# Attention and sticky-expert kernel: gate loads behind batch 0's keys, a sparse read of batch 0's keys and values at the start, batch 2's keys behind its phi

## The chip, the core and the metric

One core of one Trainium2 chip runs the kernel. The time is the device time of one execution in microseconds; of several executions the median is given. A profiled execution has a span (first to last instruction) and a time of its own that also holds what lies around the span.

## What is computed

Eight batches, eight heads, 576 tokens, head width 64, 32 memory slots; eight experts with a hidden width of 1024.

```python
a = softmax(phi, over the 576 tokens)               # [b, h, s, 32]
k_m = einsum('bhsm,bhsd->bhmd', a, k)               # 32 keys and 32 values for each head
v_m = einsum('bhsm,bhsd->bhmd', a, v)
attn = softmax(q @ k_m.T / 8)                       # [b, h, s, 32]
x = (attn @ v_m)                                    # heads side by side: [b, s, 512]
# sticky experts: token 0 takes argmax(x @ w_gate); a later token takes a fresh argmax
# where sigmoid(x @ w_local) < 0.5, else the expert of the token before
out[b, s] = p[e] * (relu(x[b, s] @ w1[e]) @ w2[e])
```

## The kernel before

The work goes batch by batch. For one batch there is an attention part (softmax of `phi`, the products with keys and values, the scores of the queries) and an expert part: the logits of the batch's first token choose one expert (`c_pl`, `c_choice`, L860 to L881), the index goes to the queue that issues transfers (`expert`, L1342), its `w1` and `w2` are loaded, `w_pg` (L1065) multiplies the batch's 32 values with `w1`, `hidden` (L1094) and `second`, `second_turned` (L1129, L1187) do the two large products. Tokens with another expert are done at the end, if there are any.

The order on every engine is written by hand. `SCHEDULE` (L41) is a list of steps, "batch name"; its first line (L42) is everything before batch 0's large products, and each later line is run at one `yield` of `moe`, so after a group of large matmuls of the batch that is then in its expert part. A step appends its instructions to the engines' queues, and each engine works in that order. In the expert part of one batch the attention part of the next is interleaved.

All transfers are issued by SyncE (SP in the profile) in the order of the steps; a transfer that has to wait for its buffer holds up what is behind it in that queue. The buffers that matter: `kv_t` (keys and values of a batch, one buffer), `q_t` (one), `phi_t` (one, and batch 1's in another place), `raw` (halves of `w1` and `w2`, three).

Steps that the change and the prediction name, with their lines:

- `phi`: 576 KB (L468); for batch 0 in two pairs of heads, `phi 0` and `phi 1`, of 288 KB (L1463). `colmax` (L561, work in L559) takes the maximum over tokens, `pm`, `mc`, `pm2`, `cx` (L593 to L618) spread it, `sub` and `exp` (L620, L625) give the weights.
- `k 0`, `v 0`, `v 1`, `k 1`: batch 0's keys and values in pieces of six and three of nine token groups (L476, `PIECES` in L450, issued by L466). `kv tile` allocates the buffer, `kv` allocates it and loads keys and values, `k` and `v` load one of them.
- `pkv a`, `pkv b` (batch 0) and `pkv 0`, `pkv 1` (L646): the products of weights with keys and values. They read keys and values together, six and three token groups in batch 0.
- `gate loads` (L413): `w_local` as 4 rows of 512 bytes into `wl`, and `w_gate` into `wg`, in pieces of 32 bytes. `gate turn` (L417): one small transpose of `wl` on TensorE and one copy into `wg` on ScalarE. `wg` is first read by `pgg` (L714).
- `fill N`, `warm`: matmuls on zeros whose result nobody reads (L535, L550).
- `q 0`, `q 1`: half the heads of a batch's queries, eight transfers of 72 KB in rows of 128 bytes (L483). `q0 b`, `q0 c`: batch 0's queries (L525).
- `w1 0`, `w1 1`, `w2 0`, `w2 1`: halves of the expert's matrices (L1031, L1043). `pg 0` needs `w1 0` and `pg 1` needs `w1 1`; `G 0`, `G 1` (L1084) split the products in two parts of lower precision on ScalarE and VectorE for `hidden`.

Of the kernel before, what the change touches and what calls it, by code (L numbers as in the profile page):

```python
# [8 lines left out]
F32 = mybir.dt.float32  # L9
# [29 lines left out]
}  # L39

SCHEDULE = """  # L41
1 warm s, 0 gate constants, 0 kv tile, 0 q0 tile, 1 warm s, 1 warm t, 0 fill 0, 0 warm f, 0 q0 a, 1 warm s, 0 phi 0, 0 phi 1, 0 colmax 0, 0 gate loads, 0 warm f, 0 k 0, 0 colmax 1, 0 pm, 0 mc, 0 warm b, 0 pm2, 0 cx, 0 dsub 0, 0 dsub 1, 0 v 0, 0 v 1, 0 exp 0, 0 exp 1, 0 warm f, 0 k 1, 0 asum 0, 0 warm f, 0 o q, 1 phi, 0 fill 7, 0 pkv a, 0 gate turn, 0 asum 1, 0 fill 1, 0 sums, 0 fill 2, 0 pkv b, 0 rinv, 0 q0 b, 0 kvn, 0 fill 3, 0 pT, 0 kvT, 0 fill 4, 0 o psc, 1 kv tile, 1 cm 0, 0 pgg, 0 o turn, 0 o mx, 0 o sub, 0 warm b, 0 o exp, 0 p q 0, 0 o sum, 0 at, 0 o inv, 0 o mul, 1 cm 1, 0 o at, 0 ggt, 0 p q 1 0, 0 p q 1 1, 0 q0 c, 0 pl0, 1 k, 1 cm 2, 0 choice, 0 fill 5, 0 p psc, 0 p turn, 0 p mx, 0 p sub 0, 0 z q 0, 0 fill 6, 0 p sub 1, 0 q0 d, 0 expert, 0 p exp 0, 0 p sum 0, 1 pm, 0 p exp 1, 0 p sum 1, 0 p inv, 0 z q 1, 0 z q 2, 0 w1 0 a, 1 mc, 0 p mul 1, 0 p at 1, 0 pg lo, 1 pm2, 0 p mul 0, 0 p ah 1, 0 Gh lo 0, 0 z psc, 0 p at 0, 0 p ah 0, 0 Gh lo 1, 0 w1 1, 1 cx, 0 Gl lo, 0 p al 1, 1 v, 0 z turn, 0 p al 0, 0 fill 9, 1 sub 1, 1 sub 0, 0 z mx  # L42
0 pg hi, 0 pg 1, 0 G hi, 0 z sub, 0 G 1, 1 exp 0, 0 z exp, 1 exp 1, 1 asum, 0 w2 0, 0 z sum, 1 q 0, 0 warm b
0 w2 1, 0 z inv, 0 z mul, 0 z at

# [8 lines left out]


0 split 5, 0 split 6, 1 z qT 1, 0 at store
2 phi, 0 g exp, 1 kvT, 1 a psc, 0 split 7, 1 pgg
1 a turn
0 g prob
1 a mx, 0 g cols, 1 a sub, 2 colmax  # L60
# [1 line left out]
2 pm, 2 mc  # L62
1 ggt, 0 evict 1
1 z psc, 1 a at, 1 z turn, 1 pl0, 1 a ah
1 choice, 1 a al, 2 kv, 2 pm2, 1 z mx, 1 z sub, 1 expert
2 z qT 0, 2 cx, 1 z exp
1 z sum
1 w1 0, 1 z inv
# [59 lines left out]
4 kv, 3 z sub, 3 expert, 3 w1 0, 4 asum, 3 z exp, 3 z sum  # L128
2 g cols, 3 z inv
3 z mul  # L130
3 z at, 2 g present, 4 a qT 0, 1 kv store, 4 q 1, 4 pkv 0, 3 w1 1, 4 pkv 1, 5 phi, 3 w2 0, 3 pg 0, 5 q 0, 4 sums, 3 g pl, 3 z ah
3 g lt, 2 evict 0, 4 rinv, 4 z qT 0, 3 g L

3 G 0, 4 kvn, 4 z qT 1, 3 z al, 4 a qT 1, 4 pT
4 kvT, 4 a psc, 2 evict 1, 3 g fresh, 4 a turn, 4 a mx, 3 pg 1, 4 pgg, 5 colmax, 4 a sub, 4 ggt, 3 g kept
# [197 lines left out]
def tile_memattn_stickymoe(  # L333
# [12 lines left out]
    nc = tc.nc  # L346
# [13 lines left out]
    const = ctx.enter_context(tc.tile_pool(name="const", bufs=1))  # L360
# [40 lines left out]
    def gate_constants():  # L401
        for e in range(E):
            nc.gpsimd.memset(code[:, e : e + 1], float(E - e))
        for i in range(2):
            nc.gpsimd.memset(ggts[i], 0.0)
            nc.gpsimd.memset(ams[i], 0.0)
            nc.gpsimd.memset(ends[i], 0.0)
            nc.gpsimd.memset(crs[i], 0.0)
            nc.gpsimd.memset(c0s[i], 0.0)
# [51 lines left out]
    def load_tokens(dst, src, heads, piece=slice(0, TN)):  # L461

        m = src.shape[2]
        ns = slice(m * piece.start, m * piece.stop)
        sv = src.rearrange("(h g) (p n) m -> (g p) h (n m)", g=NG, n=TN)
        nc.sync.dma_start(out=dst[:, heads].rearrange("p h n m -> p h (n m)")[:, :, ns], in_=sv[:, heads, ns])  # L466

    def fetch_phi(st, by_pairs=False, pool=pin, tag="phi"):  # L468
        st.pt = pool.tile([P, HG, TN, M], F32, tag=tag, name="phi_t", bufs=1)
        for hs in pairs if by_pairs else (slice(0, HG),):  # L470
            load_tokens(st.pt, phi[st.b], hs)

    def kv_tile(st):
        st.kv = pin.tile([P, 2, HG, TN, D], F32, tag="kv", name="kv_t", bufs=1)
# [864 lines left out]
    h, w = pairs  # L1339
    a, z = PARTS  # L1340
# [21 lines left out]
    def al(st, p):  # L1362
# [4 lines left out]
    STEPS = {  # L1367

        "phi": lambda st: fetch_phi(st) if st.b > 1 else fetch_phi(st, False, pf, "oT"),
        "kv": fetch_kv,  # L1370
        "kv tile": kv_tile,
# [89 lines left out]
    lo, hi = slice(0, 256), slice(256, 512)  # L1461

    def phi_pair(st, hs):  # L1463
# [4 lines left out]
    STEPS.update({  # L1468

        "gate loads": gate_loads,  # L1470
        "gate turn": gate_turn,
        "gate constants": lambda st: gate_constants(),
        "warm f": lambda st: warm(1, 1024),
# [110 lines left out]
```

## Time and profile before

| | us |
|---|---|
| median of 3 runs | 395.77 (393.54 to 396.47) |
| the profiled execution's own time | 396.51 |
| its span | 394.9 |
| TensorE matmuls busy | 385.2 |
| VectorE busy | 280.7 |
| ScalarE busy | 177.1 |
| GpSimd busy | 152.6 |

The granted TensorE clock is at full speed in the whole span. The profiled execution is 0.74 us above the median of the runs, and 1.6 us of its time lie around the span. In the rows below, PE is a matmul, PEld the load of its weights (which overlaps matmuls), DVE VectorE, ACT ScalarE, POOL GpSimd, SPq the queue that issues transfers. "Landing" counts from the start of the issue. An engine's idle time stands in brackets before the thing that ended it.

### The profile page before, as it was taken

The numbers are of one execution on the slowest core, as the hardware profiler recorded it, in microseconds if no ns is written. First come the engines' busy times: TensorE is split into PE (matmuls) and PEld (weight loads), VectorE is DVE, ScalarE is ACT, GpSimd is POOL, SyncE is SP. The second block draws the span as 40 slices with busy tenths as digits, with TensorE's granted clock in tenths as the row PEclk, the third lists the DMA queues.
The fourth block names the chain that finished last, engine by engine and source line by source line (L and its number), as shares of the span: only waits on it lengthen the run. The fifth ranks groups of instructions, "written<-read, shape, count | busy, mean of one in ns | idle before, by whom it ended". The sixth has DMA issues, their size and how long they took to land.

```text
span 394.9 us, 10791 instructions
## 1 busy us (share of the span) xinstructions
PE 385.2 (98%) x4326; PEld 333.7 (84%) x4326; DVE 280.7 (71%) x701; ACT 177.1 (45%) x437; POOL 152.6 (39%) x164
## 2 busy tenths in 40 slices
PE   8999999899999999999999999999999999999996
PEld 5667979699898976899879988799888998799886
DVE  3588798888986797875887689747745677356330
ACT  1257742437435565216461752525533653435311
POOL 1025733428125672047513931328513651057000
PEclk9999999999999999999999999999999999999999
DMA  7989979899969887999578847998580039702111
GB/s 216 341 266 272 204 161 361 235 270 224 237 227 288 212 293 184 288 340 230 192 250 230 274 140 246 352 275 216 168 297 4 2 81 325 270 0 66 29 42 57
DMA packets 115950, 82.59 MB, mean 209 GB/s; under 512 B 70132, under 2 KB 89592, under 8 KB 115896
## 3 DMA queue, kind: packets, MB, share of 16 engines
q1 hardware_dynamic: 115896, 81.86, 70.3%
q8 instruction: 35, 0.57, 0.6%
q14 instruction: 19, 0.16, 0.1%
HBM read 66.60 MB, written 15.24 MB: 207 GB/s over the span
## 4 chain that ended last, share of the span: by engine, by line
PE 52%; DMA 5%; SPq 4%; DVE 1%; issue 1%; ACT 1%; DVEq 0%
PE ph L1109 15%; PE po L1147 6%; PE po L1148 5%; PE po L1149 5%; PE po L1197 5%; PE po L1198 5%; PE po L1199 5%; DMA att_d<-at 3%; SPq L492 3%; PE pg L1076 2%; PE pkv L654 2%; DMA raw<-in_moe_w_dram 1%; PE po L1171 1%; PE psc L779 1%; PE pl L889 1%
## 5 line engine op out<-in xcount | busy, mean ns | idle before, releaser
L1062 POOL TENSOR_TENSOR w2l<-raw,w2h 128x512 fp32r<-128x512 f32 x64 | 83.2, 1323 | 59.4 <-ACT w2h L1061 40.9
L1109 PE MATMUL ph<-ah,Gh 128*128 128x256 f32 (+1 forms) x256 | 73.4, 301 | 0.6 <-DVE h L1119 0.5
L1109 PE MATMUL ph<-ah,Gl 128*128 128x256 f32 (+1 forms) x256 | 72.3, 296 | 0.2
L1197 PE MATMUL po<-h,w2l 128*128 128x320 f32 x224 | 71.0, 317 | 0.0
L1119 DVE SCALAR_TENSOR_TENSOR h<-ph,h 128x320 fp32r<-128x320 f32 (+2 forms) x104 | 52.4, 517 | 25.3 <-ACT h L1117 24.7
L1199 PE MATMUL po<-h,w2h 128*128 128x320 f32 x224 | 69.2, 309 | 0.0
L1198 PE MATMUL po<-h,w2h 128*128 128x320 f32 x224 | 69.2, 309 | 0.0
L1117 ACT ACTIVATE h<-ph 128x320 fp32r<-128x320 f32 (+1 forms) x96 | 46.7, 492 | 39.1 <-PE ph L1109 38.9
L1147 PE MATMUL po<-w2h,h 128*128 128x512 f32 (+1 forms) x152 | 58.9, 388 | 0.0
L1148 PE MATMUL po<-w2l,h 128*128 128x512 f32 (+1 forms) x152 | 57.6, 379 | 0.0
L1149 PE MATMUL po<-w2h,h 128*128 128x512 f32 (+1 forms) x152 | 57.5, 378 | 0.0
L1109 PE MATMUL ph<-al,Gh 128*128 128x256 f32 (+1 forms) x256 | 54.9, 295 | 0.0
L1109 PEld LDWEIGHTS ph<-ah,Gh 128*128 128x128 f32 x256 | 48.1, 188 | 2.5 <-DVE h L1119 1.0
L1204 POOL TENSOR_TENSOR oT<-oT,gT 128x320 f32<-128x320 f32 x28 | 21.9, 789 | 72.6 <-DVE oT L1203 56.1
L848 POOL TENSOR_TENSOR al<-at,ah 128x576 fp32r<-128x576 f32 (+1 forms) x18 | 23.1, 1291 | 67.4 <-ACT ah L844 67.4
L1109 PEld LDWEIGHTS ph<-ah,Gl 128*128 128x128 f32 x256 | 48.1, 188 | 0.6 <-DVE Gl L1091 0.6
L1061 ACT ACTIVATE w2h<-raw 128x512 fp32r<-128x512 f32 x64 | 38.1, 625 | 22.7 <-PE po L1199 14.9
L1197 PEld LDWEIGHTS po<-h,w2l 128*128 128x128 f32 x224 | 42.2, 188 | 1.8 <-issue 1.1
L1198 PEld LDWEIGHTS po<-h,w2h 128*128 128x128 f32 x224 | 42.1, 188 | 0.1
L1199 PEld LDWEIGHTS po<-h,w2h 128*128 128x128 f32 x224 | 42.1, 188 | 0.0
L1109 PEld LDWEIGHTS ph<-al,Gh 128*128 128x128 f32 x256 | 41.2, 189 | 0.0
L1147 PEld LDWEIGHTS po<-w2h,h 128*128 128x128 f32 x152 | 28.6, 188 | 6.5 <-issue 1.6
(165 smaller groups left out, 588.4 us busy)
## 6 DMA issues: line engine op xcount, KB each, us to landing
raw<-in_moe_w_dram SPq DMA_DIRECT2D x34, 512.0 KB, 6.6
raw<-in_moe_w_dram SPq DMA_DIRECT2D x15, 1024.0 KB, 7.3
kv_t<-in_k_dram SPq DMA_DIRECT2D x7, 1152.0 KB, 7.4
kv_t<-in_v_dram SPq DMA_DIRECT2D x7, 1152.0 KB, 10.7
q_t<-in_q_dram SPq DMA_DIRECT2D x112, 72.0 KB, 3.5
att_d<-at SPq DMA_DIRECT2D x8, 576.0 KB, 4.3
out_dram<-oT SPq DMA_DIRECT2D x28, 160.0 KB, 3.3
phi_t<-in_phi_dram SPq DMA_DIRECT2D x7, 576.0 KB, 6.3
```

Source lines behind the costliest of these rows:

```text
L848: (eng or nc.gpsimd).tensor_tensor(out=st.al[:, gs, ss], in0=st.at[:, gs, ss], in1=st.ah[:, gs, ss], op=ALU.subtract)
L1061: nc.scalar.activation(h, src, AF.Copy)
L1062: nc.gpsimd.tensor_tensor(out=l, in0=src, in1=h, op=ALU.subtract)
L1109: nc.tensor.matmul(pv[:, c - c0], lhsT=lt[:, g, cs], rhs=rt[:, g, s0 : s0 + n], start=(i == 0), stop=(i == 5),)
L1117: nc.scalar.activation(hc[:, :, 0:n], pv, AF.Relu)
L1119: nc.vector.scalar_tensor_tensor(out=hc[:, :, o : o + z - a], in0=pv[:, :, a:z], scalar=0.0, in1=hc[:, :, a:z], op0=ALU.max, op1=ALU.subtract,
L1147: nc.tensor.matmul(po[:, c0:c1], lhsT=h[:, c, th], rhs=hi, start=(c == 0), stop=False)
L1148: nc.tensor.matmul(po[:, c0:c1], lhsT=h[:, c, th], rhs=lo, start=False, stop=False)
L1149: nc.tensor.matmul(po[:, c0:c1], lhsT=h[:, c, tl], rhs=hi, start=False, stop=(c == FC - 1))
L1197: nc.tensor.matmul(po[:, 0:n], lhsT=lo, rhs=h[:, c, 0:n], start=(c == 0), stop=False)
L1198: nc.tensor.matmul(po[:, 0:n], lhsT=hi, rhs=h[:, c, 0:n], start=False, stop=False)
L1199: nc.tensor.matmul(po[:, 0:n], lhsT=hi, rhs=h[:, c, n : 2 * n], start=False, stop=(c == FC - 1))
```

## The change

Four edits:

1. A new step `touch`, first in the schedule. It issues two transfers from ScalarE's queue: of batch 0's keys, and of its values, 16 bytes out of every 32 KB, 36 rows each, into two small tiles that nothing reads.
2. `gate loads` goes from before `k 0` to behind `k 1`, and `gate turn` from between `pkv a` and `asum 1` to behind `kvn`, ahead of `fill 3`.
3. For batch 2, `kv` is split in `kv tile`, `k` and `v`; the buffer and the keys come right behind `2 phi`, ahead of batch 2's first queries (`2 q 0`), the values stay where `kv` was.
4. For batch 3, `pg 0` goes to the next line of the schedule, so behind `4 sums`, `3 g pl` and one more group of large matmuls.

```diff
 SCHEDULE
-1 warm s, 0 gate constants, 0 kv tile, 0 q0 tile,
+0 touch, 1 warm s, 0 gate constants, 0 kv tile, 0 q0 tile,
...
-0 phi 0, 0 phi 1, 0 colmax 0, 0 gate loads, 0 warm f, 0 k 0, 0 colmax 1,
+0 phi 0, 0 phi 1, 0 colmax 0, 0 warm f, 0 k 0, 0 colmax 1,
...
-0 v 0, 0 v 1, 0 exp 0, 0 exp 1, 0 warm f, 0 k 1, 0 asum 0, 0 warm f, 0 o q, 1 phi, 0 fill 7,
+0 v 0, 0 v 1, 0 exp 0, 0 exp 1, 0 warm f, 0 k 1, 0 gate loads, 0 asum 0, 0 warm f, 0 o q, 1 phi, 0 fill 7,
-0 pkv a, 0 gate turn, 0 asum 1, 0 fill 1, 0 sums, 0 fill 2, 0 pkv b, 0 rinv, 0 q0 b, 0 kvn, 0 fill 3,
+0 pkv a, 0 asum 1, 0 fill 1, 0 sums, 0 fill 2, 0 pkv b, 0 rinv, 0 q0 b, 0 kvn, 0 gate turn, 0 fill 3,
...
-2 phi, 0 g exp, 1 kvT, 1 a psc, 0 split 7, 1 pgg
+2 phi, 2 kv tile, 2 k, 0 g exp, 1 kvT, 1 a psc, 0 split 7, 1 pgg
...
-1 choice, 1 a al, 2 kv, 2 pm2, 1 z mx, 1 z sub, 1 expert
+1 choice, 1 a al, 2 v, 2 pm2, 1 z mx, 1 z sub, 1 expert
...
-3 z at, 2 g present, 4 a qT 0, 1 kv store, 4 q 1, 4 pkv 0, 3 w1 1, 4 pkv 1, 5 phi, 3 w2 0, 3 pg 0, 5 q 0, 4 sums, 3 g pl, 3 z ah
-3 g lt, 2 evict 0, 4 rinv, 4 z qT 0, 3 g L
+3 z at, 2 g present, 4 a qT 0, 1 kv store, 4 q 1, 4 pkv 0, 3 w1 1, 4 pkv 1, 5 phi, 3 w2 0, 5 q 0, 4 sums, 3 g pl, 3 z ah
+3 pg 0, 3 g lt, 2 evict 0, 4 rinv, 4 z qT 0, 3 g L
...
+    def touch():
+        for i, x in enumerate((k, v)):
+            t = const.tile([36, 4], F32, name=f"touch{i}")
+            nc.scalar.dma_start(out=t, in_=x[0].rearrange("h s d -> (h s d)").rearrange("(t x) -> t x", t=36)[:, 0:4])
```

## Rows read from the trace of the kernel before

**Rows 1.** The page: busy time of each engine; the chain that ended last.

```profile
PE 385.2 (98%) x4326; PEld 333.7 (84%) x4326; DVE 280.7 (71%) x701; ACT 177.1 (45%) x437; POOL 152.6 (39%) x164
PE 52%; DMA 5%; SPq 4%; DVE 1%; issue 1%; ACT 1%; DVEq 0%
```

**Rows 2.** Waits of TensorE's weight loads: total us, times, longest.

```profile
PEld pg L1076 <- DMA raw<-in_moe_w_dram: 4.1, 4, 1.8
```

**Rows 3.** Timeline of the issuing queue, first 8 us: start, us, engine, line, transfer.

```profile
2.83 0.41 SPq L414 DMA_DIRECT2D wl<-in_moe_w_local_dram  x1
3.71 0.50 SPq L466 DMA_DIRECT2D kv_t<-in_k_dram  x1
```

**Rows 4.** Transfers issued in the first 80 us: count, KB each, us to landing.

```profile
wg<-in_moe_w_gate_dram SPq DMA_DIRECT2D x1, 16.0 KB, 4.4
kv_t<-in_v_dram SPq DMA_DIRECT2D x1, 768.0 KB, 7.6
kv_t<-in_k_dram SPq DMA_DIRECT2D x1, 384.0 KB, 8.8
```

**Rows 5.** Windows of the start: length, busy by engine, clock, DMA share, GB/s.

```profile
2.75:4.75 2.00, 2.00 (x41) 1.48 (x38) 0.00 (x0) 0.00 (x0) 0.03 (x1) 1.00 0.88 261
4.75:6.75 2.00, 2.00 (x23) 1.08 (x22) 1.94 (x2) 0.00 (x0) 0.00 (x0) 1.00 0.91 177
6.75:9.75 3.00, 2.83 (x11) 1.14 (x10) 1.27 (x3) 0.28 (x1) 0.00 (x0) 1.00 1.05 383
```

**Rows 6.** Timeline of the engines, 4 to 14 us.

```profile
4.81 2.17 DVE L559 TENSOR_REDUCE cm<-phi_t 128x64 f32<-128x576 f32 x2 [3.36 <-DMA phi_t<-in_phi_dram]
...
8.69 0.28 ACT L618 ACTIVATE cx<-pm 128x128 f32<-128x128 f32 x1 [6.49 <-PE pm L612]
...
10.85 0.89 PE L555 MATMUL wp<-wz 128*128 128x32 bf16 x21
11.96 1.58 PE L654 MATMUL pkv<-kv_t,phi_t 64*32 64x128 f32 x96 [0.22 <-DMA kv_t<-in_v_dram]
...
13.48 0.13 PEld L420 LDWEIGHTS pwl<-ident,wl 4*128 4x128 f32 x1 [0.20 <-issue]
```

**Rows 7.** Timeline of the issuing queue, 48 to 65 us.

```profile
52.97 4.49 SPq L492 DMA_DIRECT2D q_t<-in_q_dram  x8
57.55 0.44 SPq L466 DMA_DIRECT2D kv_t<-in_k_dram  x1
58.04 0.51 SPq L466 DMA_DIRECT2D kv_t<-in_v_dram  x1
64.02 1.03 SPq L1040 DMA_DIRECT2D raw<-in_moe_w_dram  x2
```

**Rows 8.** Windows around these transfers, columns as in rows 5.

```profile
53.00:54.00 1.00, 1.00 (x6) 0.81 (x5) 0.96 (x4) 0.00 (x0) 0.15 (x1) 1.00 0.09 29
54.00:59.00 5.00, 5.00 (x24) 4.12 (x23) 4.86 (x11) 2.70 (x10) 0.00 (x0) 1.00 0.80 124
```

**Rows 9.** Landing of batch 2's values (issued 58.04) and batch 1's `w1 0` (64.02).

```profile
kv_t<-in_v_dram SPq DMA_DIRECT2D x1, 1152.0 KB, 9.1
raw<-in_moe_w_dram SPq DMA_DIRECT2D x1, 1024.0 KB, 7.3
```

**Rows 10.** Timeline of weight loads and VectorE, 65 to 78 us.

```profile
65.48 0.74 DVE L747 STREAM_TRANSPOSE qT<-q_t 128x576 f32<-128x576 f32 x1
...
71.31 0.18 PEld L1076 LDWEIGHTS pg<-raw,kvT 64*32 64x32 f32 x16 [1.80 <-DMA raw<-in_moe_w_dram]
...
73.12 1.29 DVE L1091 TENSOR_TENSOR Gl<-pg,Gh 128x512 fp32r<-128x512 f32 x2 [1.54 <-ACT Gh L1089]
```

**Rows 11.** Timeline around batch 3's `pg 0` and `pg 1`: weight loads, issuing queue.

```profile
152.71 0.18 PEld L1076 LDWEIGHTS pg<-raw,kvT 64*32 64x32 f32 x16 [1.12 <-DMA raw<-in_moe_w_dram]
...
161.18 0.18 PEld L1076 LDWEIGHTS pg<-raw,kvT 64*32 64x32 f32 x16 [0.69 <-DMA raw<-in_moe_w_dram]
...
155.23 0.40 SPq L1040 DMA_DIRECT2D raw<-in_moe_w_dram  x1
```

More of the change, by code (lines that the diff above doesn't have):

```diff
@@ L41 @@
 SCHEDULE = """
-1 warm s, 0 gate constants, 0 kv tile, 0 q0 tile, 1 warm s, 1 warm t, 0 fill 0, 0 warm f, 0 q0 a, 1 warm s, 0 phi 0, 0 phi 1, 0 colmax 0, 0 gate loads, 0 warm f, 0 k 0, 0 colmax 1, 0 pm, 0 mc, 0 warm b, 0 pm2, 0 cx, 0 dsub 0, 0 dsub 1, 0 v 0, 0 v 1, 0 exp 0, 0 exp 1, 0 warm f, 0 k 1, 0 asum 0, 0 warm f, 0 o q, 1 phi, 0 fill 7, 0 pkv a, 0 gate turn, 0 asum 1, 0 fill 1, 0 sums, 0 fill 2, 0 pkv b, 0 rinv, 0 q0 b, 0 kvn, 0 fill 3, 0 pT, 0 kvT, 0 fill 4, 0 o psc, 1 kv tile, 1 cm 0, 0 pgg, 0 o turn, 0 o mx, 0 o sub, 0 warm b, 0 o exp, 0 p q 0, 0 o sum, 0 at, 0 o inv, 0 o mul, 1 cm 1, 0 o at, 0 ggt, 0 p q 1 0, 0 p q 1 1, 0 q0 c, 0 pl0, 1 k, 1 cm 2, 0 choice, 0 fill 5, 0 p psc, 0 p turn, 0 p mx, 0 p sub 0, 0 z q 0, 0 fill 6, 0 p sub 1, 0 q0 d, 0 expert, 0 p exp 0, 0 p sum 0, 1 pm, 0 p exp 1, 0 p sum 1, 0 p inv, 0 z q 1, 0 z q 2, 0 w1 0 a, 1 mc, 0 p mul 1, 0 p at 1, 0 pg lo, 1 pm2, 0 p mul 0, 0 p ah 1, 0 Gh lo 0, 0 z psc, 0 p at 0, 0 p ah 0, 0 Gh lo 1, 0 w1 1, 1 cx, 0 Gl lo, 0 p al 1, 1 v, 0 z turn, 0 p al 0, 0 fill 9, 1 sub 1, 1 sub 0, 0 z mx
+0 touch, 1 warm s, 0 gate constants, 0 kv tile, 0 q0 tile, 1 warm s, 1 warm t, 0 fill 0, 0 warm f, 0 q0 a, 1 warm s, 0 phi 0, 0 phi 1, 0 colmax 0, 0 warm f, 0 k 0, 0 colmax 1, 0 pm, 0 mc, 0 warm b, 0 pm2, 0 cx, 0 dsub 0, 0 dsub 1, 0 v 0, 0 v 1, 0 exp 0, 0 exp 1, 0 warm f, 0 k 1, 0 gate loads, 0 asum 0, 0 warm f, 0 o q, 1 phi, 0 fill 7, 0 pkv a, 0 asum 1, 0 fill 1, 0 sums, 0 fill 2, 0 pkv b, 0 rinv, 0 q0 b, 0 kvn, 0 gate turn, 0 fill 3, 0 pT, 0 kvT, 0 fill 4, 0 o psc, 1 kv tile, 1 cm 0, 0 pgg, 0 o turn, 0 o mx, 0 o sub, 0 warm b, 0 o exp, 0 p q 0, 0 o sum, 0 at, 0 o inv, 0 o mul, 1 cm 1, 0 o at, 0 ggt, 0 p q 1 0, 0 p q 1 1, 0 q0 c, 0 pl0, 1 k, 1 cm 2, 0 choice, 0 fill 5, 0 p psc, 0 p turn, 0 p mx, 0 p sub 0, 0 z q 0, 0 fill 6, 0 p sub 1, 0 q0 d, 0 expert, 0 p exp 0, 0 p sum 0, 1 pm, 0 p exp 1, 0 p sum 1, 0 p inv, 0 z q 1, 0 z q 2, 0 w1 0 a, 1 mc, 0 p mul 1, 0 p at 1, 0 pg lo, 1 pm2, 0 p mul 0, 0 p ah 1, 0 Gh lo 0, 0 z psc, 0 p at 0, 0 p ah 0, 0 Gh lo 1, 0 w1 1, 1 cx, 0 Gl lo, 0 p al 1, 1 v, 0 z turn, 0 p al 0, 0 fill 9, 1 sub 1, 1 sub 0, 0 z mx
 0 pg hi, 0 pg 1, 0 G hi, 0 z sub, 0 G 1, 1 exp 0, 0 z exp, 1 exp 1, 1 asum, 0 w2 0, 0 z sum, 1 q 0, 0 warm b
@@ L1470, in tile_memattn_stickymoe @@
         "gate loads": gate_loads,
+        "touch": lambda st: touch(),
         "gate turn": gate_turn,
```

## The prediction

> **What bounds the kernel now.** I read the page first. TensorE's matmuls are busy for 98% of the span, and the chain that ended last is TensorE for more than half of its length, with transfers and the issuing queue for 9% [rows 1]. So a gain is only a place where TensorE stands still, or where it does work that nobody needs. The second view is the waits of the weight loads: TensorE's largest wait for another unit is `pg` for its `w1`, 4.1 us in four pieces, the longest 1.80 us [rows 2]. The third is the timeline, at the three places where the diff works: the first 15 us [rows 3 to 6], the time around batch 1's `pg 0` [rows 7 to 10], and batch 3's `pg 0` and `pg 1` [rows 11]. The reader is to see in each which wait ends last, and what stands right behind it.
>
> **Edits 1 and 2, the start.** Batch 0's chain is: phi lands, `colmax` starts at 4.81 as its wait for phi ends, and from there every step waits for the one before until `pkv a`; in between TensorE, between short links of the chain, does a fixed string of fills, whose last ends at 10.85 + 0.89 = 11.74. `pkv a` starts at 11.96, the 0.22 us between put down to the landing of `v 0` [rows 6], which takes 7.6 us [rows 4].
>
> The transfers have a hole. From 4.75 to 6.75 the core moves 177 GB/s, in the 3 us after that 383 [rows 5]. At 383 the same bytes would have taken 2.0 x 177 / 383 = 0.92 us, so 1.08 us are lost, just where the gate's 32-byte pieces and the first reads of `k 0` stand in the queue. Edit 2 takes the two gate transfers from there, and 3.71 - 2.83 = 0.88 us of the queue's time [rows 3]; edit 1 is aimed at the first reads. How the hole divides between them no row tells. I don't need to know: if all of it goes, `v 0` lands about 1.1 us earlier, before 10.9, but the fills end at 11.74. The load can give back 0.22 us and not more, and a fifth of the hole is enough for that.
>
> `gate turn` leaves the place between `pkv a` and `pkv b`. It costs 0.13 us there, with the 0.20 us of issue before it 0.33 at most [rows 6]; I take 0.13, since issue pauses stand before the next instruction too. `pkv b` can use it if `k 1` is there; that has the longest landing of the start, 8.8 us [rows 4], and any part of the hole brings it nearer. At its new place, behind `kvn`, TensorE waits for `kvn` anyway, and `wg` is not read before `pgg`, some 2 us later. The gate transfers now stand behind `k 1` and ahead of batch 1's phi in the queue. `w_gate` took 4.4 us [rows 4]; from an issue 3 to 4 us later than now it lands by 12, or with `k 1` near 14, and `gate turn`, behind `pkv b` and so after 14 us, is read late enough. Nothing else in that queue changes place; batch 1's phi and batch 0's queries are issued at the times of before. Start: 0.22 + 0.13 = 0.35 us.
>
> The two reads are issued from ScalarE, which has nothing to do before 8.69 (6.49 us idle, [rows 6]). The trace has no transfer from ScalarE; the nearest rows are SP's issues of small rows, 0.41 us each [rows 3], so two take 0.8 us, and even at the 4.49 / 8 = 0.56 us of a query transfer [rows 7] they are over long before 8.69. Nothing, then, on that engine. What they do to the transfers beside them is not shown; phi's 576 KB are moving at 261 GB/s from 2.75 to 4.75 [rows 5], and phi is what the chain waits for. The bounds: nothing, if a read costs an engine only its bytes (72 x 16); 1.08 us if the whole lost time of the hole moves ahead of phi; 4.4 us if phi ends as late as a transfer like the gate's, landing behind the two reads. I take nothing, the row nearest in bytes being far from filling the engines, and keep 1.08 and 4.4 for the rivals.
>
> [...]
>
> **Edit 3, batch 2's keys.** Batch 1's `pg 0` stands at 71.31 after 1.80 us of wait for `w1 0` [rows 10]. That transfer was issued at 64.02 and landed 7.3 us later, at 71.3; before it in the queue stand batch 2's values, issued at 58.04, landing at 58.04 + 9.1 = 67.1 [rows 7, 9]. So `w1 0` lands 4.2 us behind the values, and what moves the values moves it. Ahead of the values are the keys (57.55) and eight transfers of queries (52.97) [rows 7]. And ahead of these the DMA engines are nearly idle for a microsecond (share 0.09), and then, with rows of 128 bytes, busy at 0.80 for five [rows 8]. The keys put behind phi fill the first hole (0.91 us), and queries that stand in line behind them can fill the second (5 x 0.20 = 1.0 us). So the values, and `w1 0` with them, land 0.9 us earlier at least, 1.9 if both go. I take 1.9: a full queue is what the second hole lacks. `w1 0` then lands at 69.4. TensorE would have come to `pg 0` at 71.31 - 1.80 = 69.51, with the start 69.16, so 0.24 us of wait stay, and it goes on 1.9 us earlier than before, start included. VectorE is the cover of the next step: its idle time there is 1.54 us, which the products of `pg 0` end [rows 10], so with the start it can come 1.54 + 0.35 = 1.89 us earlier. Both allow 1.9.
>
> What is late instead: the queries. They are needed by a transpose at 65.48 [rows 10]. Issued at 52.97 to 57.46 they were there by about 60; with 1152 KB ahead of them, at 383 GB/s 3.1 us, by 63. That is 2.5 us in hand. The keys' buffer is free once batch 1's `pkv 1` has run, which stands many lines earlier in the schedule, so the new place adds no wait to the queue.
>
> **Edit 4, batch 3.** `pg 0` waits 1.12 us for `w1 0` at 152.71, and `pg 1` 0.69 us for `w1 1` at 161.18 [rows 11]. Edit 4 puts `pg 0` about 2 us later, so its wait goes. But nothing between the two lengthens, and `w1 1` is issued at 155.23 [rows 11] at a time that the queue and the query transfers ahead of it set, not TensorE. It lands at 161.2 as before, relative to the choice of the expert; TensorE comes 1.12 us earlier and waits 0.69 + 1.12 there. I count it as nothing. The other end is 0.86 to 1.12 us, if `w1 1` too comes earlier.
>
> **The sum.** Against the profiled execution, 396.51 us: start 0.35, batch 1 1.55, batch 3 0, so 394.6. TensorE is the bound nearly all the way behind 71 us, so the 1.9 us should arrive at the end. The profiled execution lies 0.74 us above the median of the runs (395.77), and I set the sum against that: 393.9 us.
>
> **Rivals.**
>
> *The queries stay as slow as they were* (only the 0.91 us hole is filled). For it: their pace may be set by the issue of 0.56 us each, not by the ring; against it: with a full queue the share goes to 1.05 [rows 5]. `w1 0` lands at 70.4; total 0.9 us; 394.9.
>
> *The first reads are paid ahead of phi.* [...] Phi is late by d, and the chain has no slack for it. TensorE then comes to batch 1's `pg 0` at 69.16 + d, and nothing waits there for a transfer any more, as long as d is over 0.24. The change against before is d - 2.15 us. At d = 1.08 that gives 394.7. From d = 2.15 us it decides the sign, and at the bound of 4.4 the kernel is slower: 398.0. For it: the hole shows that something in the queue at that time costs far more than its bytes. Against it: 72 reads of 16 bytes are few beside the 512 pieces of `w_gate`.
>
> *Batch 3 pays too*: 0.86 to 1.12 us more, about 393.0. Against it is the fixed issue of `w1 1`.
>
> *The read does nothing*: the hole stays in part, and the start still has its 0.35, as the gate transfers alone are more than a fifth of it. The time is the forecast's, so it has no chance of its own.
>
> **How the numbers follow.** Forecast 0.45; queries slow 0.18; phi late below 2.15 us 0.13, above it 0.12; batch 3 pays too 0.12. The runs before spread from 393.54 to 396.47 for one kernel, so I widen each case by about 1 us. A range from 392.0 to 396.4 holds all but most of the slower case and the far ends. About 1% (4 us) is what a measurement here can tell from no change. To be faster than 391.8 takes the batch 3 gain and the runs' spread together: 0.10. To be slower than 399.7 takes phi's bound and more: 0.06. Within 1%: 0.84.
>
> **What would show it.** In the profile after: GB/s near 380 from 4.75 on; `colmax` still at 4.8 (if it is later, the reads stand before phi); no DMA wait ahead of `pkv a`; batch 2's queries still landed before their transpose; `pg 0` of batch 1 with under 0.5 us of wait, and VectorE's `Gl` behind it without the 1.54; `pg 0` of batch 3 without a wait, and `pg 1` with 1.5 us or more. The forecast is wrong if phi is late, if the wait at batch 1 is over 1 us, or if the time gained at 71 us is lost again at a later `w1`.

## The result, and the profile after

| | before | after |
|---|---|---|
| median of 6 runs each, us | 395.54 (393.54 to 396.47) | 399.67 (396.95 to 399.92) |
| profiled execution, us | 396.51 | 396.95 |
| its span, us | 394.9 | 395.3 |
| TensorE matmuls busy, us | 385.2 | 384.6 |

The ratio of after to before is 1.0085 [1.0056, 1.0114]: slower by 3.4 us (the medians of the table differ by 4.1), where I forecast 1.9 us less. Ratios here and below leave out the few executions that took over 1.5% longer than the fastest of their series; medians and ranges are of all runs. The profiled execution of after is the fastest of its six, so its trace shows less of the loss than the runs do.

Some of the signs that the prediction asked for are there: phi in time, `pg 0` of batches 1 and 3 without a wait for weights. Others are not: a wait ahead of `pkv a` stays, the rate from 4.75 us on isn't near 380 GB/s, and `pg 1` of batch 3 doesn't wait. The timeline of after at the start; columns are start, duration, engine, line, operation, and in brackets the idle time ahead of it with what ended it:

```profile
0.91 0.64 ACTq L477 DMA_DIRECT2D touch<-in_k_dram  x1
1.58 0.30 ACTq L477 DMA_DIRECT2D touch<-in_v_dram  x1
1.92 1.28 ACT L624 ACT_TABLE_LOAD   x1 [1.92 <-issue]
4.75 2.17 DVE L565 TENSOR_REDUCE cm<-phi_t 128x64 f32<-128x576 f32 x2 [3.31 <-DMA phi_t<-in_phi_dram]
12.94 1.58 PE L660 MATMUL pkv<-kv_t,phi_t 64*32 64x128 f32 x96 [1.65 <-DMA kv_t<-in_v_dram]
```

`colmax` starts at 4.75 (before 4.81 [rows 6]): phi isn't late, and the two reads are issued in 0.94 us while ScalarE has nothing to do. But `pkv a` waits 1.65 us for `v 0`, not less than the 0.22 of [rows 6]. The windows of the same stretch, columns as in [rows 5], then the landing of `v 0`, and its issue in after (first) and before (second; each row holds `v 0` and `v 1`):

```profile
2.75:4.75 2.00, 2.00 (x41) 1.48 (x38) 0.00 (x0) 0.45 (x1) 0.03 (x1) 1.00 0.87 243
4.75:6.75 2.00, 2.00 (x24) 0.80 (x22) 2.00 (x2) 0.00 (x0) 0.00 (x0) 1.00 0.91 265
6.75:9.75 3.00, 2.68 (x11) 1.03 (x10) 1.67 (x4) 0.49 (x2) 0.00 (x0) 1.00 1.00 316
...
kv_t<-in_v_dram SPq DMA_DIRECT2D x1, 768.0 KB, 9.5
...
3.34 1.06 SPq L466 DMA_DIRECT2D kv_t<-in_v_dram  x2
...
4.25 1.06 SPq L466 DMA_DIRECT2D kv_t<-in_v_dram  x2
```

In this profile the hole at 4.75 is partly filled (265 GB/s for 177), and the stretches beside it lose what it gains: over the 7 us 2 x 243 + 2 x 265 + 3 x 316 = 1964 KB against 2 x 261 + 2 x 177 + 3 x 383 = 2025 before [rows 5]. `v 0` is issued 0.91 us earlier and takes 9.5 us to land instead of 7.6 [rows 4], so it lands at 12.84 instead of 11.85.

Batch 1's `pg 0`, batch 3's `pg 0` and `pg 1`, and the queue ahead of batch 1's `w1 0` (weight loads, then SyncE's queue):

```profile
70.94 0.18 PEld L1082 LDWEIGHTS pg<-raw,kvT 64*32 64x32 f32 x16 [0.19 <-issue]
155.42 0.18 PEld L1082 LDWEIGHTS pg<-raw,kvT 64*32 64x32 f32 x16 [0.37 <-DMA q_t<-in_q_dram]
160.75 0.40 PEld L1082 LDWEIGHTS pg<-raw,kvT 64*32 64x32 f32 x16
...
54.18 6.40 SPq L498 DMA_DIRECT2D q_t<-in_q_dram  x8
60.63 0.50 SPq L466 DMA_DIRECT2D kv_t<-in_v_dram  x1
65.26 1.05 SPq L1046 DMA_DIRECT2D raw<-in_moe_w_dram  x2
```

The wait of 1.80 us in [rows 10] is gone, and so is that of batch 3's `pg 0` for its weights [rows 11]. But batch 3's `pg 1`, at 160.75, has no wait in front of it, where I forecast 1.5 us or more. Nothing here is slower by 3.4 us. The trace of after names no cause of the loss, and the experiments had to look for it.

### The profile page after: what moved, and what is told of

It reads as the page before. It is cut to its first block, busy times and chain, and to the rows that moved or that the text cites. A ratio compares the mean times of both kernels' runs of the same rounds, so it can differ in the third digit from the quotient of the medians.

```text
span 395.3 us, 10791 instructions
## 1 busy us (share of the span) xinstructions
PE 384.6 (97%) x4326; PEld 333.0 (84%) x4326; DVE 280.6 (71%) x701; ACT 177.1 (45%) x437; POOL 152.6 (39%) x164
## 4 chain that ended last, share of the span: by engine, by line
PE 55%; DMA 3%; SPq 2%; DVE 1%; ACT 1%; issue 1%; DVEq 0%; ACTq 0%
PE ph L1115 13%; PE po L1203 6%; PE po L1153 6%; PE po L1205 6%; PE po L1204 6%; PE po L1155 5%; PE po L1154 5%; PE pg L1082 2%; PE pkv L660 2%; DMA raw<-in_moe_w_dram 2%; SPq L498 2%; DMA out_dram<-ot 1%; PE psc L785 1%; PE pl L895 1%; PE po L1177 1%
## 5 line engine op out<-in xcount | busy, mean ns | idle before, releaser
L1068 POOL TENSOR_TENSOR w2l<-raw,w2h 128x512 fp32r<-128x512 f32 x64 | 83.3, 1324 | 59.7 <-ACT w2h L1067 42.7
```

The lines of the kernel that those rows point to most:

```text
L1068: nc.gpsimd.tensor_tensor(out=l, in0=src, in1=h, op=ALU.subtract)
```

## The experiments

Each kernel was run 12 times, with 29 to 35 runs of the kernel before beside it on the same chip; ratios are against these, with 95% intervals. All kernels here compute what the kernel before computes.

### One edit alone, four kernels

Four theories, named in the expectations: A, the new place of the gate transfers costs; B, the reads of edit 1 cost; C, batch 2's keys ahead of the queries delay something; D, batch 3's `pg 0` costs at its new place. The diffs are the parts 1 to 4 of the change above, with the lines of the schedule cut to the steps around the edit; `s_touch` has edit 1 alone (its function is in the change above):

```diff
-1 warm s, 0 gate constants, 0 kv tile, 0 q0 tile,
+0 touch, 1 warm s, 0 gate constants, 0 kv tile, 0 q0 tile,
```

> The kernel before with edit 1 alone: the two sparse reads of batch 0's keys and values at the start. Theory A (the loss sits in the place of the gate loads; the reads cost and help nothing): within 0.3% of before, 394.5 to 396.7 us, phi's column maximum still starts at 4.8 us and the first product with the values at 11.9 to 12.1. Theory B (the reads hold up what follows them in the DMA engines): 2 to 4 us slower than before, 397.5 to 399.5, with the values of batch 0 landing about 1 us later as in the changed kernel. If the reads do what they are aimed at, the bytes moved from 4.75 to 6.75 us go from 177 to over 350 GB/s, and the time gains 0.2 us.

Measured: 399.98 us (398.41 to 401.84), 1.0068 [1.0036, 1.0100]. From 4.75 to 6.75 us its profile has 207 GB/s, so the reads hardly do what they are aimed at either.

`s_gate`, edit 2 alone:

```diff
-0 phi 0, 0 phi 1, 0 colmax 0, 0 gate loads, 0 warm f, 0 k 0, 0 colmax 1,
+0 phi 0, 0 phi 1, 0 colmax 0, 0 warm f, 0 k 0, 0 colmax 1,
...
-0 pkv a, 0 gate turn, 0 asum 1,
+0 pkv a, 0 asum 1,
```

> The kernel before with edit 2 alone: the gate transfers behind batch 0's last keys, the gate's transpose behind the normalised products. Theory A (this place costs the loss): 1.5 to 4 us slower than before, 397 to 399.5, with the first product of batch 0's weights and values starting at 12.9 us and not 11.96. Theory B (the reads are at fault): as in the prediction 0.2 to 0.35 us faster than before, 395.2, that product at 11.75.

Measured: 398.37 us (396.04 to 403.32), 1.0030 [0.9996, 1.0065]. In its profile `pkv a` starts at 12.48 us, as neither theory has it.

`s_k2`, edit 3 alone:

```diff
-2 phi, 0 g exp,
+2 phi, 2 kv tile, 2 k, 0 g exp,
...
-1 choice, 1 a al, 2 kv, 2 pm2,
+1 choice, 1 a al, 2 v, 2 pm2,
```

> The kernel before with edit 3 alone: batch 2's keys behind its phi. Theories A and B both: the wait of batch 1's first expert product goes from 1.80 us to under 0.5 and the kernel is 1.3 to 1.7 us faster than before, about 394. Theory C (the loss is behind the start, in what the earlier keys push back): no faster, or 1 to 3 us slower than before, with a new wait between 72 and 130 us.

Measured: 398.29 us (394.24 to 401.27), 1.0004 [0.9961, 1.0048].

`s_pg`, edit 4 alone:

```diff
-3 w2 0, 3 pg 0, 5 q 0, 4 sums, 3 g pl, 3 z ah
-3 g lt,
+3 w2 0, 5 q 0, 4 sums, 3 g pl, 3 z ah
+3 pg 0, 3 g lt,
```

> The kernel before with edit 4 alone: batch 3's first expert product one line later. Theories A and B, and the prediction: the wait of 1.12 us before it goes and comes back before the second product at 161 us; same time within 0.3%. Theory D (edit 4 costs the loss): 1 to 3 us slower, with a wait behind 161 us that the kernel before does not have.

Measured: 397.72 us (395.03 to 401.93), 0.9995 [0.9961, 1.0029].

What follows: edit 1 carries most of the loss, the edit that I had costed at nothing; C and D are no loss, A is open within its interval. But B, the reads, doesn't follow. Edit 1 also allocates two tiles. Each takes 32 bytes of every partition in the first pool, and every pool behind it starts 64 bytes later. The built programs' allocations show it: the buffers `raw` of `w1` and `w2` go from a multiple of 512 bytes to 64 past one, `kv_t` from 96 to 160 past one, and all others with them.

### The tiles without the reads, the reads without the moved buffers

Theory E: the moved buffers cost. Theory F: the reads, or their place in ScalarE's queue, cost. `shift64` has the two tiles and no transfer:

```diff
+        for i in range(2):
+            t = const.tile([36, 4], F32, name=f"touch{i}")
+            nc.gpsimd.memset(t, 0.0)
```

> The kernel before plus the two small tiles of edit 1, written once by GpSimd and never read; no transfer is added and no step moved. The tiles are allocated ahead of the pools, so every buffer behind them starts 64 bytes later in each partition: the buffers of w1 and w2 start at 64 and no longer at 0 modulo 512. Theory E (the loss of edit 1 is the moved buffers): 2 to 3.5 us slower than before, ratio 1.005 to 1.009, and the packets of 2048 bytes at a ninetieth percentile over 90 ns as in both kernels with edit 1, where the others have 84. Theory F (it is the two reads or ScalarE's queue): within 0.2% of before.

Measured: 399.97 us (397.06 to 401.99), 1.0078 [1.0039, 1.0117].

`touch_ns` has edit 1's reads, into a buffer of the output tiles that is there anyway and unused so early, so that `raw` and the keys start where they did:

```diff
-            t = const.tile([36, 4], F32, name=f"touch{i}")
+            t = pf.tile([36, 4], F32, tag="ot", name=f"touch{i}", bufs=2)
```

> The kernel before with the two reads of edit 1, issued by ScalarE at the same place, into a buffer that is unused at that time, so that no other buffer's address changes modulo 512. Theory E (moved buffers): within 0.2% of before. Theory F (the reads or ScalarE's queue): 2 to 3.5 us slower, ratio 1.005 to 1.009, as with edit 1 itself.

Measured: 397.84 us (393.91 to 399.90), 0.9991 [0.9952, 1.0030].

`after_ns` is all four edits with that same line:

> The changed kernel with the reads of edit 1 into that unused buffer, so all four edits without the shift of the buffers. Theory E: 2 to 3 us faster than the changed kernel, ratio to before 1.000 to 1.003. Theory F: as slow as the changed kernel, 1.007 to 1.010.

Measured: 398.49 us (395.84 to 402.64), 1.0023 [0.9989, 1.0057]. So without the shift the loss is mostly gone, and the forecast gain of 1.9 us, a ratio of 0.995, isn't there: it lies outside this interval.

`align` goes the other way. It takes three small tiles (96 bytes) out of the first pool, so that keys, queries and the attention's tiles start at a multiple of 512 bytes; `raw` keeps its place:

```diff
-    c0s = [const.tile([32, 1], F32, name=f"c0_{i}") for i in range(2)]
+    c0s = [pga.tile([32, 1], F32, tag=f"c0_{i}", name=f"c0_{i}") for i in range(2)]
...
-        cnt = const.tile([1, 1], I32, name="cnt")
+        cnt = pga.tile([1, 1], I32, tag="cnt", name="cnt")
```

> The kernel before with three tiles of 32 bytes (two choices of the first expert, one count) moved from the first pool to a later one, so that the buffers of keys and values, phi, queries and the attention result start at 0 modulo 512 and not at 96, those of w1 and w2 at 0 as before. Theory E, where alignment counts for every transfer: 1 to 3 us faster than before, keys' and values' packets of 2304 bytes shorter than 93 ns. Theory E, where it counts for the buffers of 2048-byte rows alone, and theory F: within 0.3%.

Measured: 395.84 us (393.35 to 398.06), 0.9962 [0.9927, 0.9997]. The packets of keys and values, 2304 bytes each, keep their median of 93 ns.

E holds and F falls: the two tiles alone, with no transfer, cost what edit 1 costs, and the reads without the shift cost nothing that shows.

### Which buffers

Theory G: the weights' buffers. Theory H: those of keys, values and queries. `shift_w` moves what lies behind the gate's pool, `raw` first, by 64 bytes and leaves keys and queries:

```diff
+        t = pga.tile([36, 16], F32, tag="spare", name="spare")
+        nc.gpsimd.memset(t, 0.0)
```

> The kernel before with one unused tile of 64 bytes a partition in the pool just ahead of the weight pools: the raw weights, the bf16 weights behind them, phi of the batches after the first, h and the output tiles start 64 bytes past a multiple of 512 as they do with all four edits; keys, values, queries and the attention's tiles stay where they are in the kernel before (96 past a multiple of 512). The same work is computed. Theory G (the loss is in the weight chunks: rows of 2048 bytes written 64 bytes off): ratio 1.006 to 1.009, the packets of w1 and w2 slower, the p g waits later. Theory H (the loss is in the keys, values and queries, which move from 96 to 160): ratio 0.998 to 1.002. If both share it: 1.003 to 1.005.

Measured: 399.27 us (397.53 to 404.00), 1.0059 [1.0020, 1.0099].

`shift_in` moves keys, values, queries and the attention's tiles by 64 bytes and leaves the weights' buffers, by taking two tiles of 32 bytes from the gate's pool to the first one:

```diff
-        m8 = pga.tile([1, 8], F32, tag="m8", name="m8")
+        m8 = const.tile([1, 8], F32, tag="m8", name="m8")
...
-        st.rb = pga.tile([32, 1], F32, tag="rb", name="rb")
+        st.rb = const.tile([32, 1], F32, tag="rb", name="rb")
```

> The kernel before with two small tiles of the gate (rb and m8, 32 bytes each a partition) moved from the pool of the gate into the first pool: keys, values, queries and the attention's tiles start at 160 past a multiple of 512 (before 96), the weight pools and all behind them stay at 0. The same work is computed. Theory G: ratio 0.998 to 1.002. Theory H: 1.006 to 1.009. If both share it: 1.003 to 1.005.

Measured: 397.13 us (394.65 to 401.04), 0.9997 [0.9961, 1.0033].

G holds. The edits were also tried on the layout of `align`, to see whether they gain anything where no buffer is in the way. `align_k2pg` has edits 3 and 4 on it:

> The aligned layout (keys, values and queries start at a multiple of 512, the weights too; alone 0.9962 of the kernel before) with edits 3 and 4 and without edits 1 and 2. If edit 3's gain at the first gate-up matmul of batch 1 (1.8 us in the profile before, of which the aligned kernel's profile has 0.7 left) is kept: 0.992 to 0.994. If it is given back by batch 2's first matmul, as the kernel with edit 3 alone suggests: 0.995 to 0.998. If moving the keys of batch 2 ahead delays weights: above 0.999.

Measured: 395.94 us (393.95 to 398.12), 0.9977 [0.9940, 1.0014].

`after_al` has all four, the reads' tiles as in `touch_ns`:

> All four edits, the tiles of the 16-byte reads placed in the output tiles' pool, and the aligned layout. If edits 1 and 2 are worth nothing: the same as the kernel with edits 3 and 4 in the aligned layout, within 0.002. If edit 2 gains the 0.35 us that I predicted for the start: 0.001 lower. If edit 2 costs (alone it measured 1.0030 [0.9996, 1.0065]): 0.003 higher.

Measured: 395.61 us (393.67 to 398.69), 0.9978 [0.9940, 1.0015]. Neither differs from the other, nor in a way that these intervals can tell from `align` alone. So the edits gain nothing that shows there.

### Transfers or operands, and which multiple

`shift_w` moved `raw`, which transfers write and engines read, and all that lies behind it: the weight halves and `h`, which only engines use, the output tiles, from which transfers read, and batch 1's phi. `behind` moves these and leaves `raw`, with an unused tile between them:

```diff
+        if not spare:
+            spare.append(pw.tile([36, 16], F32, tag="spare", name="spare", bufs=1))
+            nc.gpsimd.memset(spare[0], 0.0)
         raw = pw.tile([P, 4, DM], F32, tag="raw", name="raw2", bufs=3)
```

> The kernel before with one unused tile of 64 bytes a partition between the raw weights and what lies behind them: the three buffers that w1 and w2 are loaded into stay at a multiple of 512, the bf16-like weight halves, phi of the batches after the first, h and the output tiles move to 64 past one. The same work is computed. If the loss lies in the writes of the weight transfers (raw): ratio 0.998 to 1.002, and the 2048-byte packets as in the kernel before. If it lies in the operands that the engines read and write, or in the output's transfers: 1.005 to 1.008.

Measured: 397.01 us (393.05 to 402.23), 0.9972 [0.9940, 1.0004].

`raw256` moves `raw` down by 256 bytes, by taking two tiles of the gate behind the weights, `raw128` by 128 with one of them:

```diff
-        crt = pga.tile([32, 32], F32, tag="crt", name="crt")
+        crt = pw.tile([32, 32], F32, tag="crt", name="crt", bufs=1)
...
-        es = pga.tile([32, 32], F32, tag="es", name="es")
+        es = pw.tile([32, 32], F32, tag="es", name="es", bufs=1)
```

> The kernel before with two tiles of the gate (crt and es, 128 bytes each a partition) moved from ahead of the raw weights to behind the weight halves: the raw weights and the halves start at 256 past a multiple of 512, the keys, h and the output tiles stay. The same work is computed. If a multiple of 256 is enough for the weight transfers: ratio 0.998 to 1.002; if it takes 512: 1.004 to 1.008.

Measured: 397.86 us (396.50 to 400.18), 1.0001 [0.9973, 1.0030].

> As the kernel before it, with crt alone moved: the raw weights and the halves start at 384 past a multiple of 512, which is a multiple of 128 and not of 256. The same work is computed. If a multiple of 64 or 128 is enough: ratio 0.998 to 1.002. If the writes want 256 or more: 1.004 to 1.008, and the 2048-byte packets as long as with the 64-byte shift.

Measured: 399.78 us (398.12 to 402.27), 1.0070 [1.0036, 1.0104].

The loss comes with the start of `raw`: none that shows at 0 and 256 past a multiple of 512, 0.6 to 0.8% at 64 and 128 past a multiple of 256. Two rivals fall by the record. The granted clock isn't the cause: over the executions with a mean granted clock of 0.998 or more alone, the mean time of `s_touch`, `shift64`, `shift_w` and `raw128` is still 1.0052 to 1.0059 of that of before. And the engines read `raw` as fast from either start: ScalarE's `w2h` takes 624 ns on average in `raw256` and in `raw128`, GpSimd's `w2l` 1322 and 1324, a weight load of `pg` 106 and 105. What is left is the transfers' writing; that is my inference, no run changes the writing alone.

The traces carry a second sign of it. A row of `w1` or `w2` is a packet of 2048 bytes, and these make up most of the packets of that size (16,384 of 18,112). The median one takes 84 ns in every kernel; what changes is how many take 86 to 100 ns. All kernels together, the offsets from the built programs, the share counted from the packets of each profiled execution:

```
kernel       raw mod 256  keys mod 256  2048-byte packets   ratio to before
                                        of 86 to 100 ns
before            0            96             1.5%           1
s_gate            0            96             1.3%           1.0030
s_k2              0            96             1.3%           1.0004
s_pg              0            96             1.4%           0.9995
touch_ns          0            96             1.3%           0.9991
after_ns          0            96             1.7%           1.0023
behind            0            96             1.6%           0.9972
raw256            0            96             1.6%           1.0001
shift_in          0           160             1.6%           0.9997
align             0             0             1.4%           0.9962
align_k2pg        0             0             1.4%           0.9977
after_al          0             0             1.3%           0.9978
s_touch          64           160            13.6%           1.0068
after            64           160            10.4%           1.0085
shift64          64           160            12.6%           1.0078
shift_w          64            96            10.7%           1.0059
raw128          128            96            12.8%           1.0070
```

The two groups do not overlap, in the packets or in the ratios as measured; the intervals of some ratios do. For the place that is written, the starts that were tried give: at 0 and 256 past a multiple of 512, 1.3 to 1.7% of these packets take 86 to 100 ns; at 64 past one and at 384, which is 128 past a multiple of 256, 10.4 to 13.6%. Why the start counts isn't shown, nor that every packet pays: the median stays at 84 ns.

How the slower packets become 2.3 to 3.4 us stays open. All 2048-byte packets together take 106.9 us on each of the 16 engines on average in before, 107.6 in `shift_w` and 106.1 in `raw128`, so their sum doesn't explain it. Nor does TensorE's wait of the weight loads for `raw`, which the wait views of `shift64` and `behind` give as (total us, times, longest):

```profile
PEld pg L1082 <- DMA raw<-in_moe_w_dram: 4.4, 4, 1.3
...
PEld pg L1081 <- DMA raw<-in_moe_w_dram: 4.0, 4, 2.0
```

The profiled executions with `raw` in one place differ among themselves by about as much as the loss or more: the last matmul starts between 391.0 and 395.2 us in `before`, `touch_ns`, `behind`, `raw256` and `shift_in`, and between 392.6 and 394.6 in `s_touch`, `shift64`, `shift_w` and `raw128`. One profile each can't place the loss on the timeline.

## Why the prediction was wrong, step by step

**The reads of edit 1: "I take nothing".** This is the step that failed, but not by its own bounds. Edit 1 alone costs 2.7 us (1.0068 of 397.3). I weighed the queue's time and the bytes, and both did cost nothing: 0.94 us on an idle engine, `colmax` at 4.75, and 0.9991 [0.9952, 1.0030] for the reads alone. The rival of reads paid ahead of phi falls with them. What I didn't count is the other thing that the new function does: it allocates. Two tiles of 16 bytes put the weights' buffers 64 bytes off, at 0.6 to 0.8%, and that is 2.3 to 3.1 us of 397. The sum fails without them too: the 1.9 us that it adds up don't show in `after_ns`, so the terms that follow count as well. The diff shows the two `const.tile`, and no row of the profile of before says what an address is worth.

**The start: 0.22 + 0.13 us.** Not obtained. I wrote that if any fifth of the hole is filled, `v 0` comes early enough. In after the hole is partly filled (265 GB/s for 177) and `v 0` lands later (12.84 us for 11.85). In the four profiled kernels with edit 2 (`s_gate`, `after`, `after_ns`, `after_al`) the 2 us of the hole move at 300, 265, 174 and 224 GB/s, and the 7 us carry 1924 to 2027 KB, for 2025 before: what fills the hole is missing in the stretches beside it. And the 0.22 us were a lucky reading, the least of all. In the 13 profiled kernels without edit 2 that wait averages 0.97 us, in the four with it 0.88: it varies from 0.22 to 1.77 us from one profiled kernel to the next. TensorE comes to batch 0's `pg`, behind the whole start, at 25.99 us on average in the 13 and at 26.22 in the four, so neither the 0.22 nor the 0.13 arrives there. Edit 2 alone gave 1.0030 [0.9996, 1.0065], so no gain, perhaps a small loss.

**Batch 1: 1.55 us.** The wait goes, as I said, but the size is wrong. In the five profiled kernels with edit 3, `pg 0` of batch 1 waits for `w1 0` 0.84 us in one and not at all in four; in the 12 without it the wait is 0.19 to 3.15. Between the `pg 0` of batch 0 and that of batch 1 the five take 45.15 us on average, the 12 take 46.19: 1.04 us gained. From there to batch 2's `pg 0` they take 47.07 against 46.62, so 0.45 go back. Both differences are averages over few profiles that spread by 1 to 4 us. Part of what goes back is a wait that the profile of `s_k2` shows (weight loads; the second row is a longer wait at batch 3's `pg 1`, 2.92 us where [rows 11] has 0.69, in this one profile):

```profile
89.89 0.19 PEld L1109 LDWEIGHTS ph<-ah,Gh 128*128 128x128 f32 x1 [0.81 <-DVE h L1119]
...
164.45 0.18 PEld L1076 LDWEIGHTS pg<-raw,kvT 64*32 64x32 f32 x16 [2.92 <-DMA raw<-in_moe_w_dram]
```

VectorE's `h` is now what TensorE waits for: the wait moved to the engine that I had looked at only one step far, up to `Gl`. All five profiles with edit 3 have this wait between the two `pg 0`, 0.3 to 1.4 us; of the 12 without it only `behind` and `shift_w` have it, where `pg 0` of batch 1 hardly waited either (0.19 and 0.23 us). What is left, about 0.6 us or 0.15%, is less than 12 runs tell apart (1.0004 [0.9961, 1.0048]). The queue's part went otherwise than I said, too: with the keys ahead, the eight query transfers took 6.40 us to issue instead of 4.49 [rows 7]. They began 1.2 us later than before, the values were issued 2.6 us later and `w1 0` 1.2 us later; so the queue itself delayed the values by 1.4 us and `w1 0` by nothing, and `w1 0` landed in time. The hole I saw in the queue was real and was filled (share 1.03 and 1.05 where [rows 8] has 0.09 and 0.80):

```profile
53.00:54.00 1.00, 1.00 (x34) 0.66 (x34) 1.00 (x3) 0.00 (x0) 1.00 (x2) 1.00 1.03 379
54.00:59.00 5.00, 5.00 (x23) 4.07 (x23) 4.83 (x14) 1.50 (x8) 0.37 (x1) 1.00 1.05 258
```

**Batch 3: nothing.** The number is right, 0.9995 [0.9961, 1.0029], the reason isn't shown. In `s_pg` the wait for weights at `pg 0` is gone, and what its row names, after 0.36 us, is the queries' transfer from the same queue. But it doesn't come back at `pg 1`, where I forecast 1.5 us or more (weight loads; `pg 0`, then `pg 1`):

```profile
156.88 0.18 PEld L1076 LDWEIGHTS pg<-raw,kvT 64*32 64x32 f32 x16 [0.36 <-DMA q_t<-in_q_dram]
...
162.23 0.40 PEld L1076 LDWEIGHTS pg<-raw,kvT 64*32 64x32 f32 x16
```

Of the five profiled kernels with edit 4, three have no wait there (`s_pg`, `after`, `after_al`) and two wait 1.00 and 1.36 us (`after_ns`, `align_k2pg`). From batch 2's `pg 0` to this `pg 1` the five take 42.94 us on average, the 12 others 43.52, between 41.6 and 45.0: a gain of 0.6 us, if there is one, is within that spread, so calling it nothing was partly luck.

**The range and the chances.** The range was built on the two gains and on how late phi can be. A loss from a layout was no case in it, so 399.67 lies 3.3 us above its upper end. It is still within the 1% (up to 399.7) that I gave 0.84, though by none of the cases that this chance was made of.

## What to carry to other kernels

Read a diff for what it allocates as well as for what it runs: one new small tile in an early pool moves every buffer behind it, and here two of them (64 bytes, 1.0078 in `shift64`) outweighed all the steps that the diff was written for. Look at where the buffers that large transfers write start in the partition: the weights' buffers here show no loss at 0 and 256 past a multiple of 512 (`raw256`, 1.0001) and lose 0.59 to 0.78% at 64 and 384 past one (`shift_w`, `raw128`, `shift64`). Other kernels' buffers were not tried, so after any change of the tiles compare the built programs' addresses, and time the kernel if they moved; to test a new step by itself, put its tile where it moves nothing. A wait read from one profiled execution is one sample (that of `pkv a` was 0.22 to 1.77 us over 17 profiled kernels), so a gain of a fraction of a microsecond taken from it wants a second profile before it is worth an edit.

## What the runs showed of the hardware that I had not expected

- A shift of 64 bytes in the start of the three weight buffers (and of what lies behind them), with the same transfers and steps, costs 0.59% to 0.78% of the time (`shift_w`, `shift64`), and 128 bytes 0.70%; 256 bytes cost nothing (1.0001 [0.9973, 1.0030]).
- For what lies behind them, most of it read and written by engines alone, 64 bytes cost nothing (`behind`, 0.9972 [0.9940, 1.0004]).
- Keys, values and queries at 96 and 160 past a multiple of 256 are alike (`shift_in`, 0.9997 [0.9961, 1.0033]). At 0 the kernel took 0.9962 [0.9927, 0.9997], the best of all that were run, and the packets of the queries, 128 bytes each, took 12.7 ns on average instead of 14.3. The wait of the weight loads for `raw` in it:

```profile
PEld pg L1076 <- DMA raw<-in_moe_w_dram: 0.7, 2, 0.5
```

  That is 4.1 us in [rows 2], each from one profile. The interval of its ratio ends near 1, and the two kernels with edits on this layout reach it only with intervals that include 1; which of the moved buffers gives the gain was not tried.
- The 96 packets of edit 1's reads (72 of 16 bytes and 24 of 4) have a queue of their own in the profile, with 0.4% of 16 engines over the first 14 us, 0.81 us in all, beside 80.9% for SyncE's:

```profile
q1 hardware_dynamic: 3721, 3.39, 80.9%
...
q10 hardware_dynamic: 96, 0.00, 0.4%
```
